# Clustered attention and a spatial gating unit on one core: the first pair by heads, casts on ScalarE, wider weight pieces, and a new planned order

## The chip, the cores and the metric

The kernel runs on one core of one Trainium2 chip. The engines are named as the profile names them: PE is TensorE (PEld its weight loads), DVE is VectorE, ACT is ScalarE, POOL is GpSimd, SP is SyncE, which here issues nearly all DMAs. The metric is the device time of one execution, in microseconds (us), and the median of several runs counts.

## The reference

There are 4 batches, 8 heads, 768 tokens and a head width of 64. Every query and key is given to the nearest of 16 centroids of its head (by cosine), and a query attends only to keys of its own cluster. What comes out is laid side by side by heads (512 wide) and goes through a gated unit.

```python
q_assign = argmax(einsum('bhsd,hcd->bhsc', q_n, c_n));  k_assign = the same with k_n
mask = q_assign[..., :, None] == k_assign[..., None, :]
scores = where(mask, 0.125 * q @ k.T, -1e9);  attn = softmax(scores)
x = (attn @ v), heads side by side            # 4 x 768 x 512
h = relu(x @ w_in);  u, v = h[..., :512], h[..., 512:]
v_n = (v - mean) / sqrt(var + 1e-6)           # over the 512 of one token
v_s = einsum('ts,bsd->btd', w_spatial, v_n) + b_spatial
out = (u * v_s) @ w_out
```

## The kernel before

Float32 values are carried as two float16 parts, a high part (a cast) and a low part (value minus high part), and a product is the sum of three products of parts. So each tensor that PE reads takes two steps, one for each part.

**Attention** goes by pairs of heads, n = 0 to 15, four pairs to a batch. `prep(n)` loads q and k of the pair (`raw`, one buffer), makes `hq` (ACT) and `lo` (DVE, line 592), takes the logits to the centroids on PE, and turns them on DVE into one-hot rows: maximum, comparison, code, maximum, comparison, then two scalings by the penalty (lines 631 and 632) into `ohx`. The one-hot rows reach `hq` by a DMA transpose and small DMAs, for the first pair by PE and two copies on DVE and two on ACT (line 652). `shifts(n)` computes scores of the own cluster for the maximum of every row (matmuls of line 716 into one of four PSUM accumulators `acc`, maxima on DVE, line 723); the maximum comes back as three more rows of `hq` by the transposes of line 746 and the DMA of line 747. `attend(n)` has twelve score tiles, six for each head: matmuls 767 and 769, the exponential 773 and the cast 775 on ACT, the low part 776 on POOL (`pt`), and 18 value matmuls, line 781. The head's result is divided (`rc`, `xn` on DVE), split into `xhl` (ACT and POOL) and transposed by DMA into `xT`.

**The gated unit** goes by 6 tiles of 128 tokens in each batch, `mlp(b)`. `v_tile` and `u_tile` multiply `xT` by the halves of `w_in` (12 matmuls of 512 columns each, line 826). Two `v` tiles share a chain of small steps for the root (lines 859 to 864: one on POOL, five on DVE), then they are scaled (866), cast (`vn`, 867, DVE) and split (868, POOL). `s_tile` multiplies by `w_spatial` (18 matmuls), gates (887), casts (`ghl`, 888, DVE), splits (889, POOL) and transposes by DMA (`gT`, 890). `p_tile` multiplies by `w_out` (12 matmuls); ACT takes the result out (897).

**Weights** are split too. `w_in` and `w_out` come as 64-bit values of which DVE makes float32 in three shifts (lines 526 to 528) before the high part (ACT, 504) and the low part (DVE, 511). `early_weights` loads all of `w_in` in eight pieces of 512 columns, with the shifts' result in an `acc`; `late_weights` loads `w_spatial` in twelve pieces of 384 columns and `w_out` in eight of 256, with the shifts' result in an SBUF tile `top`.

**The order** of every engine's queue is fixed when the kernel is built: all steps are recorded as operations with a cost, an engine and a key, and a planner (`Plan.run`) plays them through by its costs and lets the ready operation with the lowest due time plus key go first. `due()` gives the due times from the constants DUE_0, DUE, DUE_M and others; the keys are the constants with K_ and T_. At run time every engine works its queue off in that order and waits at the head for what is not there.

## Time and profile before

| what | value |
|---|---|
| median of 3 runs | 682.45 us (677.72 to 684.44) |
| profiled execution | span 679.7 us from the first to the last instruction; no time around the span is given |
| PE busy | 630.3 us, 93% of the span |
| DVE, ACT, POOL busy | 488.5, 418.7, 429.3 us |
| mean granted clock of PE | 0.992 |

The span of the profiled execution lies 2.75 us under the median of the timed runs and inside their spread. Busy PE counts each matmul from its start to its modelled end, so PE can be busy and still not run its matmuls back to back.

### The profile page before, as it was taken

What the parts mean: (1) busy time and instruction counts of PE and PEld (TensorE: products, weight loads), DVE (VectorE), ACT (ScalarE), POOL (GpSimd) and SP (SyncE); (2) the same over time, 40 slices, a digit from 0 to 9 for tenths busy, and PEclk for the clock granted to TensorE, in tenths of its full rate; (3) what the DMA queues carried; (4) which work ended last, traced back from release to release, by engine and by line L of the source; (5) the groups of instructions that cost most, each with busy time, mean ns of one, the idle gap of its engine ahead of it and who ended that gap; (6) DMA issues with size and microseconds to landing.
All of it is one profiled execution on the core that took longest, in us unless ns stands there. A gap on an engine that the chain in (4) does not pass through costs nothing.

```text
span 679.7 us, 16791 instructions
## 1 busy us (share of the span) xinstructions
PE 630.3 (93%) x6757; PEld 376.0 (55%) x6757; DVE 488.5 (72%) x937; ACT 418.7 (62%) x685; POOL 429.3 (63%) x305
## 2 busy tenths in 40 slices
...
GB/s 156 152 105 143 186 152 201 154 153 121 171 141 190 25 70 169 114 85 139 100 149 102 130 59 59 159 51 143 21 13 32 36 45 58 88 27 31 32 93 94
DMA packets 106515, 70.49 MB, mean 104 GB/s; under 512 B 90379, under 2 KB 93126, under 8 KB 106438
## 3 DMA queue, kind: packets, MB, share of 16 engines
...
## 4 chain that ended last, share of the span: by engine, by line
PE 53%; DVE 24%; DMA 11%; ACT 5%; issue 4%; POOL 1%; SPq 1%; POOLq 0%; DVEq 0%; ACTq 0%
PE acc L826 30%; DVE nm L723 8%; PE acc L781 8%; PE acc L716 5%; PE sc L767 5%; PE sc L769 5%; DMA raw<-in_kqT_dram 4%; DMA gT<-ghl 3%; DVE lo L592 2%; ACT p L773 1%; DVE vs L675 1%; ACT pt L775 1%; DMA vraw<-in_vp_dram 1%; DVE vhl L660 1%; DMA sht<-shx 1%
## 5 line engine op out<-in xcount | busy, mean ns | idle before, releaser
L776 POOL TENSOR_TENSOR pt<-p,pt 128x768 f16<-128x768 f32 x192 | 324.2, 1712 | 97.6 <-ACT pt L775 75.3
L723 DVE TENSOR_REDUCE nm<-acc 128x1 f32<-128x512 f32 (+1 forms) x288 | 182.4, 676 | 17.6 <-PE acc L716 17.4
L773 ACT ACTIVATE p<-sc 128x768 f32<-128x768 f32 x192 | 153.8, 809 | 44.8 <-PE sc L769 33.2
L775 ACT CAST pt<-p 128x768 f16<-128x768 f32 x192 | 157.4, 832 | 13.1 <-PE acc L781 10.4
L781 PEld LDWEIGHTS <-pt 128*128 128x128 f16 x3456 | 126.0, 97 | 25.2 <-POOL pt L776 2.4
L781 PE MATMUL acc<-vhl,pt 128*128 128x65 f16 (+1 forms) x3456 | 134.4, 193 | 1.9 <-POOL pt L776 1.9
L826 PE MATMUL acc<-win,xT 128*128 128x512 f16 x576 | 131.5, 379 | 0.4 <-DVE nm L723 0.4
L716 PE MATMUL acc<-hq 80*128 80x256 f16 (+1 forms) x384 | 100.6, 343 | 18.2 <-DVE nm L723 11.7
L767 PE MATMUL sc<-hq,lo 128*128 128x512 f16 (+1 forms) x384 | 95.6, 330 | 8.5 <-ACT p L773 8.1
L826 PE MATMUL acc<-vn,wsp 128*128 128x512 f16 x432 | 99.0, 379 | 0.0
L769 PE MATMUL sc<-hq 81*128 81x512 f16 (+1 forms) x384 | 95.5, 330 | 0.1
L826 PEld LDWEIGHTS <-xT 128*128 128x128 f16 x576 | 54.8, 98 | 63.1 <-issue 1.5
L826 PE MATMUL acc<-wou,gT 128*128 128x512 f16 x288 | 66.9, 379 | 1.8 <-DMA gT<-ghl 1.8
L826 PEld LDWEIGHTS <-wsp 128*128 128x128 f16 x432 | 41.0, 98 | 46.7 <-issue 0.4
L889 POOL TENSOR_TENSOR ghl<-u,ghl 128x512 f16<-128x512 f32 x24 | 28.3, 1178 | 51.6 <-DVE ghl L888 42.8
L887 DVE SCALAR_TENSOR_TENSOR u<-acc,bsp,u 128x512 f32<-128x512 f32 x24 | 17.9, 747 | 58.5 <-PE acc L826 58.5
L716 PEld LDWEIGHTS <-hq 80*128 80x128 f16 x384 | 35.2, 100 | 40.3 <-issue 19.7
L767 PEld LDWEIGHTS <-lo 128*128 128x128 f16 x384 | 35.1, 99 | 37.5 <-issue 21.6
L769 PEld LDWEIGHTS <-hq 81*128 81x128 f16 x384 | 37.8, 98 | 26.8 <-issue 1.9
L877 ACT ACTIVATE u<-acc 128x512 f32<-128x512 f32 x24 | 14.3, 596 | 54.6 <-PE acc L826 54.6
L805 POOL TENSOR_TENSOR xhl<-xn,xhl 128x384 f16<-128x384 f32 x32 | 31.6, 989 | 23.6 <-ACT xhl L804 22.5
L826 PEld LDWEIGHTS <-gT 128*128 128x128 f16 x288 | 27.7, 97 | 33.7 <-DMA gT<-ghl 2.3
(109 smaller groups left out, 645.6 us busy)
## 6 DMA issues: line engine op xcount, KB each, us to landing
...
```

Source lines behind the costliest of these rows:

```text
L716: T.matmul(out=acc.t[:, c:c + cs.stop - cs.start], lhsT=hq.t[0:R_SH, 1, h, t * P:(t + 1) * P], rhs=hq.t[0:R_SH, 0, h, cs], start=c == 0, s ...
L723: V.tensor_reduce(out=nm.t[:, t, k:k + 1] if n == 1 else nm.t[:, t:t + n, k], in_=src, axis=AX.X, op=ALU.max, negate=True)
L767: T.matmul(out=sc.t[:, cs], lhsT=lo.t[:, h, ks], rhs=hq.t[:, 2, h, cs], start=True, stop=False)
L769: T.matmul(out=sc.t[:, cs], lhsT=hq.t[0:R_E, 0, h, ks], rhs=hq.t[0:R_E, 1, h, cs], start=False, stop=True)
L773: o = op("ACT", 0.81, lambda sc=sc, p32=p32: A.activation(out=p32.t, in_=sc.t[:, 0:S], func=AF.Exp, bias=P_LOG * LN2, scale=SC_UNIT), afte ...
L775: o = op("ACT", 0.83, lambda pt=pt, p32=p32: A.copy(out=pt.t[:, 0, :], in_=p32.t), after=[o], use=[p32], new=[pt], key=K_HI)
L776: o = op("POOL", 1.72, lambda pt=pt, p32=p32: G_.tensor_tensor(out=pt.t[:, 1, :], in0=p32.t, in1=pt.t[:, 0, :], op=ALU.subtract), after=[o ...
L781: T.matmul(out=av.t[:, t * (D + 1):t * (D + 1) + w], lhsT=lhsT, rhs=rhs, skip_group_check=True, **f)
L805: xls.append(op("POOL", 1.0, lambda xn=xn, hs=hs: G_.tensor_tensor(out=xhl.t[:, :, 1, hs], in0=xn.t, in1=xhl.t[:, :, 0, hs], op=ALU.subtra ...
L826: T.matmul(out=acc.t, lhsT=lr[m][0], rhs=lr[m][1], start=(m == 0), stop=(m == n - 1))
L887: o = op("DVE", 0.72, lambda: V.scalar_tensor_tensor(out=u32.t, in0=acc.t, scalar=bsp[:, t:t + 1], in1=u32.t, op0=ALU.add, op1=ALU.mult), ...
L889: l = op("POOL", 1.2, lambda: G_.tensor_tensor(out=ghl.t[:, 1, :], in0=u32.t, in1=ghl.t[:, 0, :], op=ALU.subtract), after=[h], use=[u32, g ...
```

## The change

It has these parts:

- The first pair is prepared head by head: logits, maxima, one-hot rows and their transpose go once for each head, so that `hq` of head 0 doesn't wait for head 1. Of the copies of q under the one-hot rows, those for `hq[:, 1]` go by heads on ACT and the other by a DMA.
- The two scalings into `ohx` move from DVE to ACT for all pairs. The casts `vn` and `ghl` move from DVE to ACT.
- The chain for the root has one DVE step less.
- `w_out` is taken in four pieces of 512 columns with the shifts' result in an `acc`, `w_spatial` in six pieces of 768. The `u` half of `w_in` is loaded with the later weights. All these later weights share one buffer `wraw` of 1024 columns (before: three for `w_in`, two of 512 columns for the rest).
- `ghl` has two buffers instead of one, `gT` three instead of two.
- The costs of some DMAs in the planner and nearly all constants have new values, and so the order is another. Of that table two lines stand in the diff.

```diff
-DUE_MAX = -17.32
+DUE_MAX = -11.24
...
+GHL_BUFS = 2
+GT_BUFS = 3
...
-    r_wraw = R(wk, "wraw", [P, 512], F32, 2)
-    r_top = R(wk, "top", [P, 256], F32, 1)
+    r_wraw = R(wk, "wraw", [P, 1024], F32, 1)
...
-            top = tops.new()
+            top = r_acc.new()
...
+    def win_jobs(hf):
+        c0 = hf * DF
+        return [(w_in[k * P:(k + 1) * P, c0:c0 + DF], lambda k=k: win[:, :, k, c0:c0 + DF], DF, WIN_LOG, True, ("win", hf)) for k in range(NCT)]
 
     def early_weights():
...
+        return weights(win_jobs(1), W_AT, W_GAP, W_KEY, r_wraw0, "SP")
...
+        weights(win_jobs(0), WU_AT, WU_GAP, WU_KEY, r_wraw, "SP")
+        jobs = [(wsT[k * P:(k + 1) * P], lambda k=k: wsp[:, :, k], S, WS_LOG, False, "wsp") for k in range(NT)]
+        jobs += [(w_out[k * P:(k + 1) * P], lambda k=k: wou[:, :, k], DM, WOUT_LOG, True, "wou") for k in range(NDT)]
+        weights(jobs, WL_AT, WL_GAP, WL_KEY, r_wraw, "SP")
...
+        heads = [(0,), (1,)] if n == 0 else [(0, 1)]
         if n == 0:
-            qa0 = [op("ACT", 0.75, lambda x=x: A.copy(out=hq.t[0:D, x], in_=hq.t[D:P, 0]), after=his, use=[hq], key=KQ) for x in (1, 2)]
+            qa0 = [op("ACT", 0.75, lambda h=h: A.copy(out=hq.t[0:D, 1, h], in_=hq.t[D:P, 0, h]), after=[his[h]], use=[hq], key=KQ) for h in range(2)]
+            qa2 = [sp(lambda: nc.sync.dma_start(out=hq.t[0:D, 2], in_=hq.t[D:P, 0]), 0.9, after=his, use=[hq], key=KQ)]
...
-        k1 = op("DVE", 0.32, lambda: V.tensor_scalar(out=ohxv[:, :, 0:2], in0=oh2(0), scalar1=PEN, scalar2=None, op0=ALU.mult), after=[o_oh, last.get("oht"), c_oh], use=[misc], key=KA)
-        k2 = op("DVE", 0.32, lambda: V.tensor_scalar(out=ohxv[:, :, 2:4], in0=oh2(1), scalar1=PEN, scalar2=-PEN, op0=ALU.mult, op1=ALU.add), after=[o_oh, last.get("oht"), c_oh], use=[misc], key=KA)
...
+            k1 = op("ACT", 0.36 - 0.1 * one, lambda f=oh2, g=ohd: A.activation(out=g(0), in_=f(0), func=AF.Copy, scale=PEN), after=[o_oh, last.get("oht"), c_oh], use=[misc], key=KO)
+            k2 = op("ACT", 0.36 - 0.1 * one, lambda f=oh2, g=ohd: A.activation(out=g(1), in_=f(1), func=AF.Copy, scale=PEN, bias=-PEN), after=[o_oh, last.get("oht"), c_oh], use=[misc], key=KO)
...
-                h = op("DVE", 0.41, lambda t=t, v=v: V.tensor_copy(out=vn[:, 0, t, :], in_=v.t), after=[o] + vn_read[t], use=[v], key=T_NRM, port=True)
+                h = op("ACT", 0.6, lambda t=t, v=v: A.copy(out=vn[:, 0, t, :], in_=v.t), after=[o] + vn_read[t], use=[v], key=T_VH)
...
-            h = op("DVE", 0.43, lambda: V.tensor_copy(out=ghl.t[:, 0, :], in_=u32.t), after=[o], use=[u32], new=[ghl], key=T_G, port=True)
+            h = op("ACT", 0.6, lambda: A.copy(out=ghl.t[:, 0, :], in_=u32.t), after=[o], use=[u32], new=[ghl], key=T_G)
```

Three places show what the new order does. The first is ACT in the first pairs, from the second load of `raw` on (before) and from the one-hot scaling of the first head on (after). Before:

```order
L586 ACTIVATE hq<-raw 128x768 x2
L589 ACTIVATE raw<-raw 128x768 x2
L652 CAST hq<-sc_108 19x768 x2
L655 ACTIVATE vhl_88<-vraw 128x12x64
L686 ACTIVATE wl_93<-w_255 2x2x65
L657 ACTIVATE vraw<-vraw 128x768
L586 ACTIVATE hq<-raw 128x768 x2
L735 ACTIVATE shx_84<-nl 128x6
L738 ACTIVATE shx_84<-nl 128x6 x2
L773 ACTIVATE p_385<-sc_108 128x768
```

After:

```order
L643 ACTIVATE ohx<-acc_111 128x6x16
L644 ACTIVATE ohx<-acc_111 128x6x16
L650 CAST hq<-sc_108 19x768
L643 ACTIVATE ohx<-acc_111 128x6x16
L644 ACTIVATE ohx<-acc_111 128x6x16
L578 ACTIVATE hq<-raw 128x768 x2
L581 ACTIVATE raw<-raw 128x768 x2
L650 CAST hq<-sc_109 19x768
L657 ACTIVATE vhl_88<-vraw 128x12x64
L688 ACTIVATE wl_93<-w_271 2x2x65
L659 ACTIVATE vraw<-vraw 128x768
L737 ACTIVATE shx_84<-nl 128x6
```

The copy of the first head's rows stood behind the casts of the second pair's load, together with that of the second head, and now stands ahead of them by itself; the shift (`shx`) moved ahead of the third pair's casts.

The second place is DVE at the first piece of `w_out`, before from the step ahead of its second shift, after from its first shift. Before:

```order
L723 TENSOR_REDUCE nm_89<-acc_110 128x1
L527 SCALAR_TENSOR_TENSOR top<-wraw,top 128x256
L592 SCALAR_TENSOR_TENSOR lo<-raw,hq 128x768
L528 SCALAR_TENSOR_TENSOR top<-wraw,top 128x256
L887 SCALAR_TENSOR_TENSOR u_3332<-acc_112,bsp,u_3332 128x512
L511 SCALAR_TENSOR_TENSOR wou<-top,wou 128x256
```

After:

```order
L523 TENSOR_SCALAR acc_112<-wraw 128x512
L584 SCALAR_TENSOR_TENSOR lo<-raw,hq 128x768
L677 TENSOR_REDUCE vs<-vraw 128x128
L524 SCALAR_TENSOR_TENSOR acc_112<-wraw,acc_112 128x512
L631 TENSOR_REDUCE mx<-acc_111 128x24
L525 SCALAR_TENSOR_TENSOR acc_112<-wraw,acc_112 128x512
L632 TENSOR_TENSOR acc_111<-acc_111,mx 128x384
L888 SCALAR_TENSOR_TENSOR u_3112<-acc_110,bsp,u_3112 128x512
L633 TENSOR_TENSOR acc_111<-acc_111,wt 128x384
L509 SCALAR_TENSOR_TENSOR wou<-acc_112,wou 128x512
```

Four steps now make 512 columns where they made 256, through PSUM instead of SBUF, and one of the four accumulators is held from the first step to the last.

The third place is DVE at the first two `v` tiles of the third batch (`a`, `y`: the chain for the root). Before:

```order
L859 TENSOR_SCALAR a<-mv 128x2
L888 CAST ghl<-u_6672 128x512
L861 TENSOR_TENSOR y_7859<-y 128x2
L862 TENSOR_TENSOR y_7859<-y_7859,a 128x2
L863 TENSOR_SCALAR y_7859<-y_7859 128x2
L675 TENSOR_REDUCE vs<-vraw 128x128
L864 TENSOR_TENSOR y<-y,y_7859 128x2
L866 TENSOR_SCALAR v_7807<-v_7807,mv,y 128x512
L866 TENSOR_SCALAR v_7833<-v_7833,mv,y 128x512
L723 TENSOR_REDUCE nm_89<-acc_111 128x1
```

After:

```order
L861 TENSOR_SCALAR a<-mv 128x2
L863 SCALAR_TENSOR_TENSOR y_7923<-y 128x2
L864 TENSOR_TENSOR y_7923<-y_7923,a 128x2
L865 SCALAR_TENSOR_TENSOR y<-y_7923,y 128x2
L677 TENSOR_REDUCE vs<-vraw 128x128
L867 TENSOR_SCALAR v_7822<-v_7822,mv,y 128x512
L867 TENSOR_SCALAR v_7900<-v_7900,mv,y 128x512
L855 BN_STATS st<-v_8017 128x6
```

The cast into `ghl` is gone from DVE, and the chain is a step shorter.

## Rows read from the trace of the kernel before

**Rows 1.** The head of the page: the span, and busy us of each engine (share of the span) with the number of instructions.

```profile
span 679.7 us, 16791 instructions
...
PE 630.3 (93%) x6757; PEld 376.0 (55%) x6757; DVE 488.5 (72%) x937; ACT 418.7 (62%) x685; POOL 429.3 (63%) x305
```

**Rows 2.** Busy time by stage: start and end of the stretch, its length, busy us of PE, PEld, DVE, ACT and POOL (number of instructions), the granted clock of PE as a share of full speed, the busy share of the DMA engines, GB/s.

```profile
34.00:142.00 108.00, 94.72 (x1408) 66.32 (x1407) 101.86 (x191) 94.08 (x158) 88.91 (x56) 0.98 0.70 151
142.00:305.00 163.00, 155.04 (x1947) 97.89 (x1944) 155.42 (x276) 121.52 (x207) 125.35 (x82) 1.00 0.58 125
305.00:470.00 165.00, 163.89 (x1744) 97.06 (x1741) 129.53 (x238) 104.90 (x174) 107.32 (x74) 1.00 0.50 107
470.00:485.00 15.00, 12.52 (x92) 7.01 (x91) 12.38 (x17) 8.02 (x11) 7.57 (x5) 0.77 0.39 90
485.00:589.00 104.00, 104.00 (x1074) 61.05 (x1071) 42.31 (x89) 60.81 (x95) 71.75 (x51) 1.00 0.18 40
```

**Rows 3.** The timeline of the start: start us, duration us, engine, line, operation, tiles, count, and in brackets the idle time before it and what ended it.

```profile
9.29 0.96 DVE L592 SCALAR_TENSOR_TENSOR lo<-raw,hq 128x768 f16<-128x768 f32 x1
...
15.33 0.85 PE L635 MATMUL sc<-id,ohx 128*128 128x128 f16 x6
...
15.84 1.57 ACT L586 ACTIVATE hq<-raw 128x768 f16<-128x768 f32 x2 [3.37 <-DMA raw<-in_kqT_dram]
...
18.90 1.60 ACT L652 CAST hq<-sc 19x768 f16<-19x768 f32 x2
...
19.75 2.32 PE L716 MATMUL acc<-hq 80*128 80x512 f16 x6 [3.57 <-ACT hq L652]
...
20.39 3.08 DVE L723 TENSOR_REDUCE nm<-acc 128x1 f32<-128x512 f32 x5 [2.18 <-PE acc L716]
...
28.97 1.57 ACT L586 ACTIVATE hq<-raw 128x768 f16<-128x768 f32 x2 [6.66 <-DMA raw<-in_kqT_dram]
...
34.33 0.81 ACT L773 ACTIVATE p<-sc 128x768 f32<-128x768 f32 x1 [3.47 <-PE sc L769]
```

**Rows 4.** Groups of instructions by line and shape: count, busy us in all, mean ns of one, and the idle time ahead of them.

```profile
L592 DVE SCALAR_TENSOR_TENSOR lo<-raw,hq 128x768 f16<-128x768 f32 x30 | 41.2, 1377 | 3.4 <-ACT hq L586 3.4
...
L888 DVE CAST ghl<-u 128x512 f16<-128x512 f32 x24 | 18.9, 786 | 32.2 <-DMA gT<-ghl 32.0
...
L867 DVE CAST vn<-v 128x512 f16<-128x512 f32 x24 | 14.8, 653 | 0.0
...
L847 ACT ACTIVATE v<-acc 128x512 f32<-128x512 f32 x24 | 14.0, 594 | 37.2 <-PE acc L826 19.5 <-POOL vn L868 17.7
...
L511 DVE SCALAR_TENSOR_TENSOR wsp<-wraw,wsp 128x384 f16<-128x384 f32 x12 | 10.3, 858 | 1.4 <-ACT wsp L504 1.4
...
L511 DVE SCALAR_TENSOR_TENSOR wou<-top,wou 128x256 f16<-128x256 f32 x8 | 8.9, 1111 | 0.9 <-ACT wou L504 0.8
...
L528 DVE SCALAR_TENSOR_TENSOR top<-wraw,top 128x256 uint32<-128x256 uint32 x8 | 7.1, 888 | 0.1
...
L527 DVE SCALAR_TENSOR_TENSOR top<-wraw,top 128x256 uint32<-128x256 uint32 x8 | 6.4, 795 | 0.0
...
L526 DVE TENSOR_SCALAR top<-wraw 128x256 uint32<-128x256 uint32 x8 | 5.9, 744 | 0.0
...
L631 DVE TENSOR_SCALAR ohx<-acc 128x192 f16<-128x192 f32 x16 | 5.6, 348 | 0.1
...
L528 DVE SCALAR_TENSOR_TENSOR acc<-vn,acc 128x512 uint32<-128x512 uint32 x8 | 5.4, 678 | 0.0
```

**Rows 5.** Who PE waited for between 34 and 305 us: us in total, times, the longest.

```profile
PE sc L767 <- ACT p L773: 8.1, 18, 1.1
PE acc L716 <- DVE nm L723: 6.9, 20, 0.7
```

**Rows 6.** The timeline of PE in a stretch without a wait, for the price of matmuls back to back (columns as in rows 3).

```profile
578.15 1.25 PE L781 MATMUL acc<-vhl,pt 128*128 128x65 f16 x36
579.25 0.49 PE L767 MATMUL sc<-hq,lo 128*128 128x512 f16 x2
...
579.90 0.49 PE L767 MATMUL sc<-hq,lo 128*128 128x512 f16 x2
...
596.33 17.00 PE L826 MATMUL acc<-win,xT 128*128 128x512 f16 x78
```

**Rows 7.** The timeline around 474 us: DVE, then PE (columns as in rows 3).

```profile
470.09 0.43 DVE L888 CAST ghl<-u 128x512 f16<-128x512 f32 x1 [1.46 <-DMA gT<-ghl]
...
471.80 1.57 DVE L863 TENSOR_SCALAR y<-y 128x2 f32<-128x2 f32 x1
...
474.89 2.32 DVE L866 TENSOR_SCALAR v<-v,mv,y 128x512 f32<-128x512 f32 x2
...
477.86 0.59 PE L716 MATMUL acc<-hq 80*128 80x512 f16 x1 [2.48 <-DVE nm L723]
```

**Rows 8.** The timeline of the end: DVE, then PE (columns as in rows 3).

```profile
668.60 0.43 DVE L888 CAST ghl<-u 128x512 f16<-128x512 f32 x1 [1.32 <-DMA gT<-ghl]
...
673.43 2.76 PE L826 MATMUL acc<-wou,gT 128*128 128x512 f16 x12 [1.83 <-DMA gT<-ghl]
```

**Rows 9.** What DMA issues on SP waited for, over the whole span: us in total, times, the longest. L521 issues the loads of `w_in` and `w_out`.

```profile
SPq L521 <- DVE top L528: 9.5, 2, 8.5
...
SPq L521 <- DVE acc L528: 5.9, 1, 5.9
```

More of the change, by code (lines that the diff above doesn't have):

```diff
@@ L52 @@
 MM = 6
[L53 to L108 removed]
+W_KEY = 39.02
+WL_KEY = 33.98
+WU_KEY = 11.6
+WU_AT = 109.09
+WU_GAP = 8.81
+WL_AT = 69.05
+WL_GAP = 4.42
+W_AT = 57.96
+W_GAP = -36.25
+PREP_KEY = 13.33
+AV_KEY = 1.1
+K_SC = 11.08
+K_MX = -1.18
+K_MAX = 5.03
+TBL = 0.185
+K_SH = -40.3
+K_EXP = -100.66
+K_HI = -25.82
+K_LO = 161.1
+K_RC = 2.89
+K_XD = -29.01
+K_X = -35.23
+K_VT = -29.14
+K_G = -66.37
+KP0 = -8.82
+KC = -230.91
+T_LO = 4.55
+T_QA = 17.5
+T_OH = 6.67
+T_VH = 126.21
+T_LG = -126.86
+T_AM = -49.58
+T_OT = -3.67
+T_ROW = 14.27
+T_V = -13.63
+T_SV = 23.5
+T_VA = 2.23
+T_SA = 37.55
+T_SB = 1.67
+T_UO = 2.53
+T_PO = 47.91
+T_CONT = -98.96
+T_BN = -10.16
+T_NRM = -3.1
+T_VL = -197.16
+T_G = -39.45
+T_GL = -79.29
+T_O = 92.53
+T_B1 = 6.31
+T_B2 = 11.85
+T_B3 = 14.47
+T_Q1 = -2.89
+T_Q2 = -1.35
+T_Q3 = -3.86
+T_Q0 = -3.63
+T_Z0 = -3.86
+T_Z1 = -5.36
+T_Z2 = 17.86
 LO_POOL = (1,)
+LO0_POOL = ()
 VL_POOL = (0, 1)
 SUM_PE = tuple(range(4))
[L112 removed]
 O_BUFS = 1
+GHL_BUFS = 2
+GT_BUFS = 3
 class Ring:
@@ L631, in prep @@
-        k1 = op("DVE", 0.32, lambda: V.tensor_scalar(out=ohxv[:, :, 0:2], in0=oh2(0), scalar1=PEN, scalar2=None, op0=ALU.mult), after=[o_oh, last.get("oht"), c_oh], use=[misc], key=KA)
-        k2 = op("DVE", 0.32, lambda: V.tensor_scalar(out=ohxv[:, :, 2:4], in0=oh2(1), scalar1=PEN, scalar2=-PEN, op0=ALU.mult, op1=ALU.add), after=[o_oh, last.get("oht"), c_oh], use=[misc], key=KA)
-        if n == 0:
-            tp = r_sc.new()
-            tr = op("PE", 0.4, lambda: [T.matmul(out=tp.t[:, t * P:(t + 1) * P], lhsT=ohx[:, t].rearrange("p x c -> p (x c)"), rhs=id16, start=True, stop=True) for t in range(NT)], after=[k1, k2, c_id], new=[tp], cols=S, key=KP)
-            last["oht"] = tr
-        else:
-            tr = last["oht"] = sp(lambda: nc.sync.dma_start_transpose(oht.t, ohx.rearrange("p t x c -> p (t x c)")), 0.67, after=[k1, k2], new=[oht], turn=True, key=KP + T_OT)
@@ L639, in prep @@
-        rows = []
-        for x in range(4) if n else (0, 2, 1, 3):
-            m = (C if n else R_END - R_OH) if x > 1 else C + 1
-            def dst(x=x, m=m):
-                return hq.t[R_OH:R_OH + m, x // 2, x % 2, :]
-            def src(x=x, m=m):
-                if n == 0:
-                    return tp.t[2 * x * C:2 * x * C + m, 0:S]
-                return oht.t[2 * x * C:2 * x * C + m].rearrange("c t s -> c (t s)")
-            if n == 0:
-                rows.append(op(("DVE", "ACT")[x // 2], 0.9, lambda dst=dst, src=src, x=x: (V.tensor_copy, A.copy)[x // 2](out=dst(), in_=src()), after=[tr, lg] + qa0, use=[hq, tp], key=KR))
-            else:
-                rows.append(sp(lambda dst=dst, src=src: nc.sync.dma_start(out=dst(), in_=src()), 0.1, after=[tr, lg] + qa0, use=[hq, oht], key=KR))
+        ohxv = ohx.rearrange("p t (x e) c -> p t x e c", e=2)[:, :, :, 0, :]
@@ L688, in prep @@
         w2 = sp(lambda: nc.sync.dma_start(out=mw.t[R_E + 1:R_E + 2, :, 0:D + 1], in_=wl.t[0:1, :, 0:D + 1]), 0.05, after=[l_, c_mean], use=[wl, mw], key=KS)
-        X["rows"] = [(rows if n else rows[2 * h:2 * h + 2]) + qa0 for h in range(2)]
-        X["go"] = rows + qa0 + [qa1, lo1]
+        X["rows"] = [rows[2 * h:2 * h + 2] + [qa0[h]] if n == 0 else rows + qa0 for h in range(2)]
+        X["go"] = [x + qa2 + [qa1, lo1] for x in X["rows"]]
         X["v"] = [o_vh, o_vl, w1, w2]
@@ L769, in scores @@
                         T.matmul(out=sc.t[:, cs], lhsT=hq.t[0:R_E, 0, h, ks], rhs=hq.t[0:R_E, 1, h, cs], start=False, stop=True)
-                o = last["sc"] = op("PE", 0.66, scores, after=X["go"] + [X["shift"][h], last.get("sc")] + exps[-2:-1], use=[hq, lo], new=[sc], cols=2 * S, key=K_SC)
+                o = last["sc"] = op("PE", 0.66, scores, after=X["go"][h] + [X["shift"][h], last.get("sc")] + exps[-2:-1], use=[hq, lo], new=[sc], cols=2 * S, key=K_SC)
                 o = op("ACT", 0.81, lambda sc=sc, p32=p32: A.activation(out=p32.t, in_=sc.t[:, 0:S], func=AF.Exp, bias=P_LOG * LN2, scale=SC_UNIT), after=[o, m_half], use=[sc], new=[p32], key=K_EXP)
```

192 lines of the change are left out of this document (70 added, 122 removed).

## The prediction

> **What bounds the kernel now.** I read the head of the page first: PE is busy for 93% of the span, DVE for 72% [rows 1]. That average hides two regimes, which the table by stage shows [rows 2]. From 34 to 305 us DVE is the full engine: 101.86 of 108 us and 155.42 of 163, while PE stands still for 13.3 and 8.0. From 305 to 470 DVE is at 129.53 of 165 and PE at 163.89; from 485 to 589 PE never stops. So the second half is bound by PE, and only the first half, the start, one disturbance and the end can give time.
>
> How much idle the first half hides follows from prices of matmuls back to back [rows 6]: a matmul of 512 columns takes 17.00/78 = 0.216, a score tile 0.65 (start of one to start of the next), a block of 18 value matmuls 0.55 (36 in 1.25 less the last one's tail). Counted in PE's order between the last values of pair 3 (142 us) and of pair 8 (305 us), before has 58 score tiles, 60 value blocks, 90 blocks for maxima and 234 matmuls of the gated unit: 37.7 + 33 + 19.4 + 50.5, and about 7 of small ones, 147.6 us. The stretch lasts 163, so some 15 us are slack; PE's waits say for whom: the exponential on ACT (8.1 from 34 to 305) and the maxima on DVE (6.9) [rows 5].
>
> **The change, part by part.** The order's counts are mine; durations are from the rows.
>
> *Start.* Today the first maximum's matmul waits for the copies of both heads' rows (18.90 to 20.50, the matmul at 19.75); they stand on ACT behind casts of pair 1, which waited until 15.84 for their load [rows 3]. By heads: `lo` of head 1 ends at 10.25, the first head's one-hot is the seventh of ten half steps (0.35 as line 631, which has the same 192 elements) and ends at 12.7, two scalings at ACT to about 13.4, the transposes 0.85, a copy 0.8: 15.1, so 4.6 earlier [rows 3, 4]. But the first exponential (34.33) stays behind the casts of pair 2 on ACT, whose load landed at 28.97 with casts of 1.57 [rows 3]. `raw` has one buffer and comes free no sooner, and on SP a copy into `hq` now goes ahead of this load. I put the first exponential at 31.3: **3.0 us gained**, bounds 0 and 4.6.
>
> *Pairs 0 to 3 (34 to 142).* DVE does 7 weight steps of 0.68 less (24 for 31, `u` half later), 12 one-hot scalings of 0.35 less and, by the new order, 5 maxima of 0.62 more [rows 3, 4]: -4.8 - 4.2 + 3.1, so 96 for 101.9. ACT takes those scalings (14 with the halves; no row has one on ACT; between the 0.35 of DVE and, above, the 0.594 of an ACT step on 512 columns; I take 0.35 for a full one, it is the nearer size) and one cast less: 94.1 + 3.8 = 98. ACT is then the fuller engine. At today's filling of the fullest, 101.86/108 = 0.943, 98 needs 104: **4 gained**, bounds -4 (ACT's 14 us of idle all stay) and 6.
>
> *Pairs 4 to 8 (142 to 305).* DVE loses 10 scalings (3.5), 6 casts `vn` at 0.653 (3.9), 3 casts `ghl` at 0.786 (2.4); `w_out` goes from 19 steps of 0.74 to 1.11 (16.6) to 16 of 0.68 (10.9); `w_spatial` from 12 at 0.858 (10.3) to 6 at 1.38, as `lo` of the same shape (8.3) [rows 4]. It gains 7 more steps of `w_in` (4.8). Steps of other pairs and tiles that change sides make about -2.4. In all -15: 140 us. PE gets more to do there: 56 score tiles, 60 blocks, 86 for maxima, and 408 matmuls of the gated unit for 234, 182 us by the same prices. So DVE goes from 95% to 77% of the stretch, PE has filler, and the bound turns over to PE, as from 305 to 470 where DVE at 78.5% left PE 1.1 us idle [rows 2]. Of 15 us of slack I let 4 stand: **11 gained**, bounds 0 and 15. The cover is that filler; without it the freed DVE time buys nothing. An `acc` is now held through a piece of `w_out`, which is in the 4 that I leave.
>
> The `vn` and `ghl` casts cost ACT 0.594 each where an undisturbed DVE cast takes 0.43 [rows 4, 7]. The Trainium skill, page "ScalarE: Activation LUTs", section "Rules for kernel authors", says to keep plain arithmetic on VectorE, being faster per element there; undisturbed, the trace agrees. By that rule the 16 casts up to pair 8 would cost 2.6 us more engine time, and the stage would gain some 3 less. But the mean of the casts on DVE is 0.786 and 0.653 here [rows 4], for DVE works beside a busy POOL, and DVE is the full engine, so I don't take it.
>
> *The disturbance at 474.* A cast `ghl` waits 1.46 on DVE for the one buffer, which a transpose still reads; behind it the small step L863 takes 1.57 and the scalings 2.32, and PE waits 2.48 for a maximum [rows 7]. The stage's granted clock falls to 0.77 [rows 2]: (1 - 0.77) x 15 = 3.4 us, as 6.9 us at the lower level of 1.2 GHz, after PE had stood still for 2.48. Together 5.9. With two buffers, the cast on ACT and a chain without L863 all but POOL's neighbourhood is gone: **5 gained**, bounds 0 and 5.9.
>
> *The end.* The last cast waits 1.32 for the same buffer, and PE 1.83 for the last `gT` [rows 8]. The cast on ACT takes 0.17 longer: **1 gained**, bounds 0 and 1.8.
>
> *New stalls.* An order written anew has places of its own like that at 474; there is one in some 340 us today. I charge one: **5 lost**, bounds 0 and 12.
>
> Other edits cost nothing visible: the chain's step less is off PE's path except at 474; third `gT` and larger pieces lie beside PE's filler.
>
> Sum: 3 + 4 + 11 + 5 + 1 - 5 = 19. From the span of 679.7 that is 660.7; the median lies 2.75 above the span, so **663 us**, 2.8% faster.
>
> **The rivals.** *ACT takes DVE's place.* For: from 34 to 142 it is at 94.08 already [rows 2], its queue gets waits on DVE's chains ahead of exponentials, and PE waits for those longest [rows 5]. Against: its share falls to 121.52 of 163 afterwards. Then pairs 0 to 3 lose 4 and pairs 4 to 8 gain half: 3 - 4 + 5.5 + 5 + 1 - 5 = 5.5, or 677.
>
> *One `wraw` buffer blocks SP (slower).* Each of the 14 later loads (4 + 6 + 4) must wait until the one before is landed and read, at the head of SP's queue, with the shift's transposes behind it. Two loads waited 9.5 us in all, the longer 8.5, and another 5.9 [rows 9]; the shifts' due time moved from -17.32 to -11.24, so 6 us of lead that covered such a wait are gone. If three loads hold SP for 5.9 where no lead is left, PE loses 18; with no gain from pairs 0 to 8, 4 remain: 682.45 - 4 + 18 = 696. It decides from the second bare hold on. Against: the loads start earlier, and the first use of `w_spatial` comes more than a pair after its last piece in DVE's order.
>
> *All slack goes.* Every upper end, no new stall: 4.6 + 6 + 15 + 5.9 + 1.8 = 33, or 649. For: stages after 305 have next to none [rows 2].
>
> That the change doesn't do what it says can only be at the start, where the third load sets the exponential; that is the lower end there.
>
> **How the numbers follow.** Chances: the forecast 0.60, ACT as the bound 0.17, SP blocked 0.10, all slack gone 0.13. A measurement of this kernel can't tell changes under about 1% from none. The forecast and the last case are faster; ACT as the bound lies within 1% for the most part; SP blocked is slower. That makes 0.75, 0.14 and 0.11. The range goes from 648, the last case, to 683, which takes in the ACT case with the lower ends of the start and the disturbance; outside stay SP blocked and little else.
>
> **What would show it.** Right: the first exponential at 30 to 32; the last values of pair 3 by 136; from there to pair 8's end PE idle under 4 us and DVE under 85% of the stretch; no clock below 1.00 between 300 and 600; PE's last wait for `gT` under 1 us. Wrong: ACT busy over 95% with PE waiting for exponentials (first rival), SP standing at `wraw` loads while PE waits for scores (second), or a new stall of 10 us and more in the second half.

## The result and the profile after

The changed kernel takes 661.76 us (661.38 to 662.23 in four executions) against 681.12 (677.72 to 684.44, four) for the kernel before on the same chip: 0.9729 of its time, 95% interval 0.9684 to 0.9774. The forecast was 663.0. The profiled execution took 662.23, its span is 660.5. Of the experiments, one of e10's four executions took 1622.92 us and is left out of its median.

The head of the page after, and the shares of the chain of work that ended last, by engine (answers to [rows 1]):

```profile
span 660.5 us, 16716 instructions
...
PE 623.7 (94%) x6763; PEld 374.4 (57%) x6763; DVE 423.6 (64%) x828; ACT 446.7 (68%) x757; POOL 426.2 (65%) x305
...
PE 75%; DVE 12%; issue 6%; ACT 4%; DMA 1%; POOL 1%; POOLq 0%; SPq 0%; ACTq 0%; DVEq 0%
```

DVE lost 65 us of work, ACT took 28. The stages (columns as in [rows 2]; 137.7 is the end of pair 3's last values, 330 that of pair 8's):

```profile
34.00:64.00 30.00, 25.28 (x375) 17.13 (x373) 24.07 (x46) 21.59 (x41) 18.73 (x13) 0.93 0.56 133
64.00:137.70 73.70, 67.08 (x1055) 47.80 (x1052) 72.25 (x133) 71.12 (x123) 69.25 (x43) 1.00 0.73 169
137.70:330.00 192.30, 187.81 (x2081) 112.39 (x2080) 148.03 (x272) 138.41 (x240) 132.76 (x90) 1.00 0.56 127
330.00:476.00 146.00, 146.00 (x1700) 90.71 (x1697) 98.23 (x177) 110.91 (x186) 106.62 (x74) 1.00 0.49 107
476.00:590.00 114.00, 113.89 (x1123) 66.04 (x1121) 43.16 (x97) 69.96 (x112) 73.59 (x54) 1.00 0.20 42
```

From 64 to 137.7 DVE is still the full engine (98%, with ACT at 96.5%). From there to 330 it is at 77%, PE stands 4.5 us in 192, and from 330 to 590 it stands for 0.1.

Where the time came from can't be read by comparing pairs, since the new order puts 174 more matmuls of the gated unit ahead of pair 8's end. So I compared the traces at equal work: for a moment of the changed kernel I added up the columns of all matmuls that PE had started, and looked up when the kernel before had started as many.

| the changed kernel at | share of all columns | before at | lead, us |
|---|---|---|---|
| 30.6 (first exponential) | 1.2% | 35.5 | 4.9 |
| 64.2 (end of pair 0) | 4.9% | 62.7 | -1.5 |
| 137.7 (end of pair 3) | 15.0% | 144.7 | 7.0 |
| 330.0 (end of pair 8) | 45.5% | 343.9 | 13.9 |
| 455 | 66.1% | 469.3 | 14.3 |
| 480 | 70.3% | 500.2 | 20.2 |
| 650 | 99.2% | 669.4 | 19.4 |

The lead at the start is gone by the end of pair 0, some 1.6 us of it at a stretch from 45.3 to 48.7 us in which the granted clock is 0.50 (see e8); 8.5 come from pairs 1 to 3 (1.8 of them because the kernel before had a stretch of 3.4 us at the lower clock there, at 68 us), 6.9 from pairs 4 to 8, 5.9 at the disturbance, and the end takes 0.8 back.

### The profile page after: what moved, and what is told of

Its sections match the earlier page's. It is cut to its first block, busy times and chain, and to the rows that moved or that the text cites. A ratio compares the mean times of both kernels' runs of the same rounds, so it can differ in the third digit from the quotient of the medians.

```text
span 660.5 us, 16716 instructions
## 1 busy us (share of the span) xinstructions
PE 623.7 (94%) x6763; PEld 374.4 (57%) x6763; DVE 423.6 (64%) x828; ACT 446.7 (68%) x757; POOL 426.2 (65%) x305
## 4 chain that ended last, share of the span: by engine, by line
PE 75%; DVE 12%; issue 6%; ACT 4%; DMA 1%; POOL 1%; POOLq 0%; SPq 0%; ACTq 0%; DVEq 0%
PE acc L828 38%; PE acc L783 13%; PE sc L769 7%; PE sc L771 7%; DVE nm L725 7%; PE acc L718 6%; ACT p L775 2%; ACT pt L777 1%; DMA raw<-in_kqT_dram 1%; PE acc L613 1%; PE acc L614 1%; DMA gT<-ghl 1%; PE acc L612 1%; DVE mx L631 1%; POOL pt L778 1%
## 5 line engine op out<-in xcount | busy, mean ns | idle before, releaser
L828 PE MATMUL acc<-win,xT 128*128 128x512 f16 x576 | 129.1, 379 | 0.5 <-DVE nm L725 0.5
L718 PE MATMUL acc<-hq 80*128 80x256 f16 (+1 forms) x384 | 96.3, 335 | 8.6 <-DVE nm L725 7.0
L828 PE MATMUL acc<-vn,wsp 128*128 128x512 f16 x432 | 97.6, 379 | 0.0
L889 ACT CAST ghl<-u 128x512 f16<-128x512 f32 x24 | 14.8, 618 | 52.0 <-DVE u L888 52.0
L718 PEld LDWEIGHTS <-hq 80*128 80x128 f16 x384 | 33.0, 99 | 24.4 <-issue 10.1
```

What stands on the lines that cost most here:

```text
L718: T.matmul(out=acc.t[:, c:c + cs.stop - cs.start], lhsT=hq.t[0:R_SH, 1, h, t * P:(t + 1) * P], rhs=hq.t[0:R_SH, 0, h, cs], start=c == 0, s ...
L828: T.matmul(out=acc.t, lhsT=lr[m][0], rhs=lr[m][1], start=(m == 0), stop=(m == n - 1))
```

## The experiments

In all but e5 the order of the kernel that the experiment starts from was written out as a list and replayed, so that one part is changed and every other instruction keeps its place in its queue; an instruction that must wait for one further down the list moves behind it. Line numbers in rows of these kernels are shifted. The sets ran on other chips; the kernel before had medians of 677.71, 678.40, 678.11 and 677.34 there. The changed kernel ran on the first chip alone, where the kernel before took 681.12, so a comparison of times with 661.76 goes across chips. Variants are still compared with it directly, for e4 and e8, which differ from it least, gave 661.92 and 661.31 in two of these sets, and e4's trace runs 0.1 to 0.2 us beside the changed kernel's from pair 0 to the end. Where it matters the neighbour in the same set is named too.

### e1 and e2: single parts in the kernel before

```diff
-    r_ghl = R(moe, "ghl", [P, 2, DF], F16, 1)
-    r_gT = R(moe, "gT", [P, 2 * NDT, P], F16, 2)
+    r_ghl = R(moe, "ghl", [P, 2, DF], F16, 2)
+    r_gT = R(moe, "gT", [P, 2 * NDT, P], F16, 3)
```

> The kernel before with its own order of instructions on every engine, word for word, and only two buffers for ghl (for one) and three for gT (for two). Theory 1 (the stall near 474 us hangs on the one buffer: the cast waits 1.46 us, behind it the small step and the scalings come late, PE stands 2.48 us and then runs 6.9 us at the lower clock level): no wait of the cast for a transpose there, no stage with a granted clock below 1.00 near 474, 4 to 6 us faster than before, so 675 to 677. Theory 2 (the neighbourhood of POOL slows the small step and the scalings, whatever the cast does): at most 1.5 us faster, and the granted clock still falls after 470.

675.95 us, 0.9966 of before (0.9941 to 0.9991). The stage of the disturbance, then the cast and the small step on DVE:

```profile
470.00:485.00 15.00, 14.86 (x166) 9.44 (x164) 14.87 (x24) 12.68 (x20) 11.12 (x7) 1.00 0.41 83
```
```profile
467.64 0.42 DVE L932 CAST ghl<-u 128x512 f16<-128x512 f32 x1
...
469.97 1.50 DVE L907 TENSOR_SCALAR y<-y 128x2 f32<-128x2 f32 x1
```

The cast waits no more, PE is busy 14.86 of 15 us for 12.52 in [rows 2], and the clock stays at 1.00, although the small step still takes 1.50. At equal work the lead rises from 0.9 to 6.3 us there, as theory 1 says. But the median gains 1.8 only, and 11 of the 19 executions of the kernel before in this set have a mean clock of 0.997 or more, where 6.8 us at 0.50 would leave 0.995: most of them don't pay this stall in full. Its size was a property of the execution that was profiled. And since an execution of the kernel before can go without it, one profile of each doesn't show that the buffers alone took it away: e2, with one `ghl` buffer and the casts off DVE, has a clock of 1.00 there too.

```diff
-h = op("DVE", 0.43, lambda: V.tensor_copy(out=ghl.t[:, 0, :], in_=u32.t)
+h = op("ACT", 0.6, lambda: A.copy(out=ghl.t[:, 0, :], in_=u32.t)
```

(and the same for `vn` and the two scalings)

> The kernel before with its own order, and the casts of vn and ghl and the one-hot scalings on ACT, each in the place that its old time gives it; nothing else of the change. Theory 1 (from 34 to 305 us DVE is the full engine, so what is taken from it shows at once): DVE's busy time from 142 to 305 falls from 155 to some 146 and the run is 4 to 8 us faster, 674 to 678. Theory 2 (the new order, which brings 174 more matmuls of the gated unit ahead of pair 8's end, is what fills PE; the casts alone only move the wait from DVE to ACT): within 1.5 us of before.

680.03 us, 1.0029 of before (1.0006 to 1.0052). Two of the stages of [rows 2], and the group of `ghl` casts on ACT:

```profile
142.00:305.00 163.00, 153.11 (x1893) 96.16 (x1892) 148.17 (x254) 125.80 (x223) 121.53 (x81) 1.00 0.56 123
305.00:470.00 165.00, 160.54 (x1733) 95.60 (x1732) 115.17 (x210) 111.80 (x194) 103.29 (x73) 1.00 0.47 104
```
```profile
L932 ACT CAST ghl<-u 128x512 f16<-128x512 f32 x24 | 14.8, 617 | 45.2 <-DMA gT<-ghl 28.3 <-DVE u L931 16.9
```

DVE is 7 us freer from 142 to 305, and PE does no more for it (153.11 for 155.04). ACT now stands 28.3 us at the head of its queue for the one `ghl` buffer, with exponentials behind. Freeing DVE in this way is worth nothing in the old order with one `ghl` buffer; both edits together in that order were not run.

### e3, e4 and e11: single parts taken out of the changed kernel

e3 puts the casts and scalings back on DVE (e2's edit reversed).

> The changed kernel with its own order, and the casts of vn and ghl and the one-hot scalings back on DVE, each in its place. Theory 1 (freed DVE time is a good part of the gain): pairs 0 to 3 lose 2 to 3 us, since DVE is busy 72 of 74 us there already, pairs 4 to 8 another 2 to 3: 665 to 668. Theory 2 (PE's filler hides what DVE does from pair 4 on, and the scalings cost DVE no more than the wait for ACT): within 1.5 us of the changed kernel, 660 to 663.3.

665.02 us, 0.9807 of before (0.9752 to 0.9863), 3.3 slower than the changed kernel and 3.1 slower than e4 in the same set: theory 1, at its lower end. From 138 to 330, the changed kernel first, then e3:

```profile
138.00:330.00 192.00, 187.51 (x2079) 112.21 (x2078) 147.72 (x271) 138.10 (x240) 132.46 (x90) 1.00 0.56 127
```
```profile
138.00:330.00 192.00, 187.90 (x2080) 112.88 (x2079) 156.56 (x302) 129.71 (x214) 132.89 (x91) 1.00 0.56 129
```

8.8 us more on DVE change nothing for PE in this stage: filler hides them, as theory 2 says for it. In the profiled execution 1.9 us were lost by 158 us, ahead of the first cast `vn` (166.1), so none of it is the casts'; its first exponential comes at 32.40 for 30.64, with the scalings on DVE. Some 1 comes back by 210, and 1.5 go again between 330 and 570, where the casts can be the cause.

```diff
-        heads = [(0,), (1,)] if n == 0 else [(0, 1)]
+        heads = [(0, 1)]
```

> The changed kernel with its own order, and the first pair's one-hot codes made for both heads in one piece again (one group of logits, five steps, two scalings, one group of transposes) in the place of the second head's. Theory 1 (the start's 3.7 us, seen at the first exponential, are not carried: the second pair's maxima start at 39.6 us for 40.0 before, since that pair's codes are no earlier): the first exponential falls back to 32.5 to 34.5, the second pair's first maximum stays within 1 us of 39.6, and the end is within 1 us of the changed kernel, 661 to 663. Theory 2 (the start is carried to the end): 3 to 4 us slower, 665 to 666.

661.92 us, 0.9778 of before (0.9711 to 0.9844). ACT at the start, the changed kernel first, then e4:

```profile
15.50 0.79 ACT L650 CAST hq<-sc 19x768 f16<-19x768 f32 x1 [0.98 <-PE sc L647]
...
16.59 1.58 ACT L578 ACTIVATE hq<-raw 128x768 f16<-128x768 f32 x2
...
30.64 0.81 ACT L775 ACTIVATE p<-sc 128x768 f32<-128x768 f32 x1 [0.49 <-PE sc L771]
```
```profile
16.02 0.79 ACT L701 CAST hq<-sc 19x768 f16<-19x768 f32 x1 [0.92 <-PE sc L696]
...
30.75 0.81 ACT L826 ACTIVATE p<-sc 128x768 f32<-128x768 f32 x1
```

The end is where theory 1 put it, but its own number for the start was wrong too: the first exponential moved by 0.1 us, not by 2 to 4. Making the codes by heads is worth nothing that can be measured (the copies of the rows still go by heads in e4). The timelines say what brought the first exponential from 34.33 [rows 3] to 30.64: on ACT the first row copy now stands ahead of the second pair's four casts (15.50 and 16.02 for 18.90 before), and the shift ahead of the third pair's (25.10 for 30.45). The scalings on ACT have a part in it, for e3 without them has 32.40. No run took the order on ACT back alone.

```diff
-GHL_BUFS = 2
-GT_BUFS = 3
+GHL_BUFS = 1
+GT_BUFS = 2
```

> The changed kernel with its own order, and one buffer for ghl and two for gT as in the kernel before. Theory 1 (in the new order, too, the cast of the next tile would wait for the transpose of the last, now on ACT with exponentials behind it): waits of 1 us and more on ACT at the casts of ghl, and 1 to 4 us slower, 663 to 666. Theory 2 (with MLP tiles spread evenly the buffers are idle long enough): within 1 us, 660.8 to 662.8.

672.46 us, 0.9886 of before (0.9842 to 0.9931): 10.7 slower, far beyond theory 1. One row of who ACT waited for (us, times, longest), which the changed kernel doesn't have:

```profile
ACT ghl L934 <- DMA gT<-ghl: 21.9, 5, 6.8
```

At equal work 13.5 us go between 245 and 299 us, in pair 7: the cast holds ACT, and the exponentials and casts `pt` behind it come late. PE then waits 6.3 us, and after that its granted clock is down:

```profile
PE acc L828 <- POOL pt L823: 6.3, 3, 3.6
```
```profile
266.00:283.10 17.10, 14.68 (x94) 8.64 (x95) 7.91 (x15) 8.77 (x15) 8.93 (x7) 0.50 0.15 38
```

By estimate the lower clock costs half of the 14.68, which is 7.3, and with the 6.3 that makes the loss. Two buffers that are worth 1.8 us in the old order carry 10.7 in this one, which was planned with them; a new order for one buffer was not tried.

### e5, e6 and e7: the order

```diff
-DUE_PREP = -73.77
-W_AT = 57.96
+DUE_PREP = -59.83
+W_AT = 71.02
```

(and every other number that both tables have)

> The changed code with every number of the table that both kernels have set to its value in the kernel before, so that the order is planned from the old numbers; the eight that only the changed kernel has, and all its casts, scalings, pieces and buffers, stay. Theory 1 (the new table is more than half of the gain: the parts alone gave about 2 us with the buffers and 3 us with the casts): 668 to 674. Theory 2 (the parts make the gain and any sensible order of them does): within 2 us of the changed kernel, 660 to 664.

690.53 us, 1.0186 of before (1.0158 to 1.0214). Every other part of the change is in it, and it is 12 us slower than before and 29 slower than with its own table (29 slower than e8 in the same set, too). From 64 to 300 us PE waits 11.3 us for exponentials, the changed kernel 4.8:

```profile
PE sc L769 <- ACT p L775: 11.3, 18, 2.5
```
```profile
PE sc L769 <- ACT p L775: 4.8, 11, 0.8
```

The parts need a table that fits them; how much of the 29 is this table's merit and how much the old one's misfit, the run can't say.

```diff
-        weights(win_jobs(0), WU_AT, WU_GAP, WU_KEY, r_wraw, "SP")
+        weights(win_jobs(0), WU_AT, WU_GAP, WU_KEY, r_wraw0, "SP")
```

(and the place of these instructions in the list)

> The changed kernel with its own order for all but one part: the u half of w_in (four pieces: loads, twelve steps and four lo steps on DVE, four casts on ACT) stands where the kernel before has it in time, right behind the v half and through the same three buffers. Theory 1 (from 64 to 138 us DVE is busy 72.25 of 73.7, so 7 to 8 steps of 0.6 to 0.68 us more show one to one there, and pairs 4 to 8 get less back, since PE bounds them): 3 to 5 us slower, 665 to 667. Theory 2 (DVE's steps for weights slip into its idle time, and the third pair's end stays): within 1 us of the changed kernel, 661 to 663.

669.18 us, 0.9872 of before (0.9839 to 0.9906): 7.4 slower than the changed kernel, 7.9 slower than e8 in the same set, theory 1 but more of it. At equal work the loss lies between 114 and 162 us, 7.6 us, where 7 to 8 steps of 0.68 make 5. PE and DVE at 142 us show a part of the rest:

```profile
142.11 0.38 PE L763 MATMUL acc<-hq 80*128 80x512 f16 x1 [0.78 <-DVE nm L770]
143.27 0.38 PE L763 MATMUL acc<-hq 80*128 80x512 f16 x1 [0.78 <-DVE nm L770]
```
```profile
142.52 0.69 DVE L770 TENSOR_REDUCE nm<-acc 128x1 f32<-128x512 f32 x1 [0.47 <-PE acc L763]
143.68 0.69 DVE L770 TENSOR_REDUCE nm<-acc 128x1 f32<-128x512 f32 x1 [0.47 <-PE acc L763]
144.29 0.68 DVE L554 SCALAR_TENSOR_TENSOR win<-acc,win 128x512 f16<-128x512 f32 x1
```

Matmul and maximum wait for each other in turn, 1.16 us for one maximum of 0.69: one of the four `acc` is left for them, another is held by the piece of `w_in` until 145.0. So a weight piece costs its steps and, on top, the `acc` that it holds. How much of the 2.6 that is can't be told from the run, for the granted clock is 0.50 here from 134.6 to 138.0 and from 144.9 to 148.3.

```diff
-order of the 24 instructions of w_out: casts wou on ACT from 224.2 to 255.1
+order of the 24 instructions of w_out: casts wou on ACT from 306.7 to 337.1
```

> The changed kernel with its own order for all but one part: the four pieces of w_out (loads and steps) stand 85 us later, so that the last is ready at about 340 us as in the kernel before (345) and not at 256; the output projections of the first batch can only follow it. Theory 1 (what filled PE in pairs 4 to 8 are the 174 more matmuls of the gated unit that an early w_out lets run there): PE idle comes back there, and the run is 4 to 8 us slower, 666 to 670. Theory 2 (DVE's relief does it, and the filler may as well run later): within 1.5 us of the changed kernel, 660 to 663.3.

683.96 us, 1.0086 of before (1.0057 to 1.0115): 22.2 slower than the changed kernel, 22.7 slower than e8 in the same set. From 225 to 345 us, the changed kernel, then e7:

```profile
225.00:345.00 120.00, 119.64 (x1261) 70.47 (x1258) 80.95 (x151) 83.26 (x143) 76.22 (x53) 1.00 0.58 126
```
```profile
225.00:345.00 120.00, 109.36 (x1159) 64.69 (x1158) 80.02 (x148) 77.04 (x132) 72.75 (x50) 0.96 0.46 109
```

DVE does the same work in both, two thirds of the stage; PE stands 10.6 us and does 102 matmuls less. So theory 1: what fills PE in pairs 4 to 8 is work that exists because `w_out` is ready, and a free DVE alone is not the gain. In the kernel before the first output projection started at 345.8 us, in the changed one at 257.9. But the 22.2 are not all for want of filler. At equal work 10 go between 249 and 289 us, where value blocks wait for POOL's `pt` and the clock is at 0.50 from 260.2 to 267.0. The other 11 to 12 go between 307 and 365, where the late projections stand in a heap and PE waits for them:

```profile
337.73 14.34 PE L873 MATMUL acc<-wou,gT 128*128 128x512 f16 x57 [2.02 <-ACT wou L553]
355.13 4.45 PE L873 MATMUL acc<-wou,gT 128*128 128x512 f16 x12 [3.06 <-DMA gT<-ghl]
```

Whether the filler needed the freed DVE isn't shown: with 8.8 us more on DVE (e3) PE lost nothing in this stage.

### e8, e9 and e10: where the lead of the start went

```diff
+                    for _ in range(14):
+                        T.matmul(out=r_sc.tiles[1][:, 0:512], lhsT=id16, rhs=hq.t[:, 0, 0, 0:512], start=True, stop=True)
...
-                    for t, cs, c in parts:
+                    for t, cs, c in parts * (2 if twice else 1):
```

> The changed kernel with its own order, and more for PE at the start whose results are not used: 14 matmuls of 512 columns into a free score buffer behind the first logits (where PE stood 3.7 us), and each of the nine groups for the first head's maxima done twice over. In the changed kernel the granted clock was at the lower level from about 21.4 to 35.1 and 45.3 to 48.7 us. Theory 1 (the low clock lies beside waits for DVE and ACT and costs nothing; runs of the changed kernel at a mean clock of 0.987 and 0.994 had the same time): within 1 us, 660.8 to 662.8, whatever the clock does. Theory 2 (the low clock is what took back the 3.7 us of the start): the granted clock is 1.00 in the first 60 us and the run is 2 to 4 us faster, 658 to 660.

661.31 us, 0.9755 of before (0.9725 to 0.9785): by time theory 1, though the clock didn't do what theory 2 asks for. PE by stretches of 3 us (its busy time, granted clock, DMA share, GB/s): full from 12 to 15, where the changed kernel has 0.34, and yet at the lower level of 1.2 GHz from 30 to 33 (28.3 to 35.1 in all).

```profile
12.00:15.00 3.00, 3.00 (x9) 1.00 0.97 294
...
30.00:33.00 3.00, 3.00 (x11) 0.50 0.59 121
```

Up to 34 us the clock costs nothing that these traces show. The changed kernel and e11, whose order is the same up to there, were at 0.75 and 0.73 from 9 to 34; e7 was at 1.00, and yet it stands 0.4 us behind the changed kernel at the first maximum (19.34 for 18.92) and still 0.3 behind it at 44 us. First e11, then e7:

```profile
9.00:34.00 25.00, 18.28 (x141) 10.67 (x138) 21.89 (x43) 14.07 (x27) 8.04 (x5) 0.73 0.67 175
```
```profile
9.00:34.00 25.00, 19.02 (x147) 10.95 (x147) 21.89 (x44) 14.74 (x28) 7.60 (x5) 1.00 0.65 172
```

Behind that it does cost. In the changed kernel the granted clock is 0.50 from 45.3 to 48.7, with PE busy throughout; in e7 and e11 it is 1.00 there. Two rows of the same maxima on DVE stand around this stretch, in the changed kernel and then in e7:

```profile
45.30:48.70 3.40, 3.40 (x26) 2.11 (x26) 2.66 (x7) 1.58 (x2) 0.00 (x0) 0.50 0.33 65
```
```profile
44.54 2.04 DVE L725 TENSOR_REDUCE nm<-acc 128x1 f32<-128x512 f32 x3
52.72 0.68 DVE L725 TENSOR_REDUCE nm<-acc 128x1 f32<-128x512 f32 x1
```
```profile
44.85 1.87 DVE L770 TENSOR_REDUCE nm<-acc 128x1 f32<-128x512 f32 x3
51.39 0.68 DVE L770 TENSOR_REDUCE nm<-acc 128x1 f32<-128x512 f32 x1
```

Ahead of it the changed kernel leads by 0.3, behind it it lags by 1.3: 1.6 us lost, and against e11 and e12 it is 1.6 as well. That is most of what moves the end of pair 0 (64.2 in the changed kernel; 61.8, 62.9 and 63.0 in e11, e7 and e12). From there on the gap stays as it is: at the end of pair 3 these three are 2.4, 1.3 and 1.2 ahead, e11 is still 2.4 ahead at the end of pair 6 and e12 1.2 at the end of pair 15. So what is gained by the end of pair 0 is carried through, though DVE and ACT are 96 to 98% busy behind it.

Not all of the lead gets there: e7 has its first exponential 3.3 us ahead of the kernel before (31.06 for 34.33) and its end of pair 0 only 1.0 ahead (62.9 for 63.9), with no low clock in either. The trace shows one reason: DVE stands still before the third pair's logits, with the second pair's maxima behind them. In the changed kernel:

```profile
39.82 0.56 DVE L631 TENSOR_REDUCE mx<-acc 128x24 f32<-128x384 f32 x1 [3.56 <-PE acc L614]
```

```diff
-PE: ... score tile, value block, third pair's logits, maxima, maxima ...
+PE: ... third pair's logits, maxima, maxima, score tile, value block ...
```

> The changed kernel with its own order but for three groups on PE: the third pair's logits and the first two of the second pair's maxima stand ahead of the score tile and the value block that they followed (DVE stood still from 36.3 to 39.8 us there, waiting for these logits, which waited behind value blocks for POOL). Theory 1 (at the start the end of pair 0 is set by when DVE gets its next work, not by the first exponential): the wait of 3.6 us on DVE falls to 1 to 1.5 us, the third pair's end comes 1 to 2.5 us earlier than 137.7 and the run is 1 to 2 us faster, 659.5 to 661. Theory 2 (PE and ACT set the pace there and DVE's wait was beside them): within 0.5 us of the changed kernel.

663.27 us, 0.977 of before (0.9725 to 0.9815): 1.5 slower than the changed kernel, which neither theory said.

```profile
37.37 0.56 DVE L676 TENSOR_REDUCE mx<-acc 128x24 f32<-128x384 f32 x1 [1.98 <-PE acc L659]
```

The wait fell from 3.56 to 1.98, pair 0 ended at 62.4, the lead of 1.8 us held to the end of pair 2 (111.7 for 113.5) and was lost in pair 3 (137.5 for 137.7). There the granted clock is down with PE busy throughout:

```profile
119.20:122.60 3.40, 3.40 (x26) 1.93 (x25) 2.92 (x5) 3.40 (x8) 2.62 (x2) 0.50 0.49 111
```

The changed kernel is at 1.00 there, and e8, which also falls to 0.50 from 120.5 to 123.9, loses 1.5 us at the same place. So up to 119 us the profiled execution speaks for theory 1, at half of its price (0.9 of the 1.8 stood at the first maximum already, 18.05 for 18.92, ahead of the edit), and then the clock took that back. Why the median lies above that execution (662.09) isn't shown; the mean clocks of the four, 0.982 to 0.990, are on the whole below those of the changed kernel, 0.987 to 0.994.

```diff
-            if n in LO_POOL or (n == 0 and h in LO0_POOL):
+            if n in LO_POOL and h:
+                plan.seq += 1
+            elif n in LO_POOL:
```

(and 28 places in the list)

> The changed kernel with its own order but for the second pair's codes: lo of its second head on DVE straight from the load (for a cast on ACT and a subtraction on POOL), its logits, the five steps, the two scalings and the transpose ahead of the last five of the first pair's first nine maxima, and its own first maxima some 2 to 4 us earlier on PE and DVE. Theory 1 (the start's gain was lost because the second pair's codes were no earlier than in the kernel before): the second pair's first maximum comes at 35 to 38 us for 40.3, the first exponential 2 to 3 us later, and the run is 0 to 2.5 us faster, 659 to 662. Theory 2 (the first exponential is what counts after all): 2 to 3 us slower, 664 to 665.

664.71 us, 0.9778 of before (0.9727 to 0.983). By time that is theory 2, but the edit didn't do what it was to do: the second pair's first maximum came at 39.25 (expected 35 to 38), because DVE waited 2.04 us for its matmul. It says nothing for either theory, save that this order isn't better.

### e12: the end

```diff
-            o32 = r_o32.new()
+            o32 = (r_v32 if b == B - 1 and t == NT - 2 else r_o32).new()
```

(and the store behind the next copy in the list)

> The changed kernel with its own order, but at the very end the store of the last tile but two is issued behind the copy of the next tile (which goes to a free v buffer so that it needn't wait for the store), some 2 to 3 us later. In the changed kernel this store was issued at 650.25, 0.5 us behind the end of POOL's part of the last ghl (649.78), and the two transfers ran side by side from 651.0 to 653.4; PE waited 1.9 us for the last gT. Theory 1 (the store takes transfer time from the last transpose, which is why the end gained nothing though the wait for the ghl buffer is gone): PE's last wait falls to 1.0 to 1.4 us, and the end comes 0.5 to 0.9 us earlier. Theory 2 (the transpose takes that long by itself): the wait stays at 1.8 to 2.0.

660.39 us, 0.9754 of before (0.9713 to 0.9796). The end of the changed kernel, then of e12:

```profile
648.62 1.16 POOL L890 TENSOR_TENSOR ghl<-u,ghl 128x512 f16<-128x512 f32 x1 [5.32 <-ACT ghl L889]
...
650.25 0.40 ACTq L899 DMA_DIRECT2D out_dram<-o  x1
...
654.10 2.76 PE L828 MATMUL acc<-wou,gT 128*128 128x512 f16 x12 [1.92 <-DMA gT<-ghl]
```
```profile
647.47 1.16 POOL L935 TENSOR_TENSOR ghl<-u,ghl 128x512 f16<-128x512 f32 x1 [5.32 <-ACT ghl L934]
...
651.06 0.34 ACTq L944 DMA_DIRECT2D out_dram<-o  x1
...
651.78 2.76 PE L873 MATMUL acc<-wou,gT 128*128 128x512 f16 x12 [0.76 <-DMA gT<-ghl]
```

From POOL's end to PE's start it is 4.32 us with the store 0.47 behind POOL's end, 3.15 with the store out of the way. Theory 1, and a little more than it expected: the wait falls to 0.76, the end gains 1.2 us. PE's row is 2.3 us earlier than in the changed kernel; the other 1.2 is the lead that this execution has from the end of pair 0 on (see e8) and not the edit's. This version has the lowest median of all, but its interval overlaps that of the changed kernel.

## Why the prediction was right, and where its steps were wrong

**The sum** of 19 met the 19.4 of the profiled execution, with errors that cancel. By the borders of the prediction's terms and at equal work: start 4.9 for 3, pairs 0 to 3 2.1 for 4, pairs 4 to 8 6.9 for 11, disturbance 5.9 for 5, end -0.8 for 1, no new stall of its own for the 5 lost, and 0.4 in between. That the time met the forecast within 1.3 us is luck in part: 663 adds 2.75 to the span where the profiled execution lies 1.7 above its own, and on the other chips the kernel before takes 677 to 678, against which 661.76 would be a gain of 16 only. Two slips in the working change nothing: 17.00/78 is 0.218 and not 0.216, and the ACT case with the two lower ends comes to 685 and lies outside the range.

**Start.** The first exponential came at 30.64 (30 to 32 forecast, 31.3 in the sum), so the size was right. The cause named, going by heads, is not: e4 has the same time without it, and the order on ACT and the scalings there are what the timelines show. What the term lacked is what comes behind it, for by the end of pair 0 the lead is -1.5: DVE stands 3.56 us for the third pair's logits (e9), and in the profiled execution 1.6 us go at the low clock.

**Pairs 0 to 3.** DVE's work from 34 us on was to be 96 and is 96.3 (24.07 and 72.25). But ACT was to be the fuller engine with 98 and has 92.7 (21.59 and 71.12), and that the filling of the fullest stays at 0.943 failed: from 34 to 64 us DVE is busy 24.07 of 30, where the kernel before has 28.54 of 29.9 up to its end of pair 0. So the term's 2.1 is made of 6.4 lost up to the end of pair 0 and 8.5 gained behind it, neither of them forecast, and each kernel loses some 1.7 at a stretch at the lower clock, the changed one at 45 us, the one before at 68. The end at 137.7 missed the mark "by 136". The sign for the first rival, ACT over 95% with PE waiting for exponentials, does show from 64 to 137.7 (96.5%, PE waits 3.9 us), but not its price.

**Pairs 4 to 8.** That filler is what PE lacked holds, by e7. DVE's share came out as said, 77%; that the filler needed it so low isn't shown (e3 has it at 82% and PE as full). The size failed at the slack: 15 us by back-to-back prices, of which the trace showed 8.0 as idle time [rows 2]. The other 7 were matmuls that take longer in this mixture than those prices say, and they still do: 6.9 were gained, with 4.5 idle left (under 4 forecast).

**The rule against casts on ACT.** The casts take 0.618 on ACT (the undisturbed one on DVE took 0.43 [rows 7]), as this group of the changed kernel shows:

```profile
L889 ACT CAST ghl<-u 128x512 f16<-128x512 f32 x24 | 14.8, 618 | 52.0 <-DVE u L888 52.0
```

The Trainium skill's rule, page "ScalarE: Activation LUTs", section "Rules for kernel authors", to keep plain arithmetic on VectorE, holds here for the single undisturbed instruction. The trace of the kernel before shows what its mean of 0.786 on DVE hides: 14 of the 24 `ghl` casts took 0.42 to 0.43 us, with POOL idle or at work beside them for 0.2 at most, and eight took 1.13 to 1.86 with POOL at work all along. The small step L863 takes 0.17 or, in the same way, 1.09 to 1.58. For the kernel as a whole the runs don't decide: with the scalings, casts on DVE cost 3.3 us (e3), but the larger part of that is lost before the first of them runs, and in the order of before moving them brought nothing (e2).

**Disturbance.** Right in size for the execution profiled, and in cause as far as e1 shows it; no granted clock below 1.00 came between 49 and 659 us. Too large for the median, where e1 gained 1.8.

**End.** The buffer wait of 1.32 went, as said. PE's last wait was still 1.92 (under 1 forecast): the last transpose now met a store, which I hadn't looked for (e12). In the kernel before the store had been issued 0.57 ahead of POOL's end, and POOL's end to PE's start was 3.18. The term lacked the question what the released transfer runs into.

**New stalls.** None of 5 us came. By e11 the second `ghl` buffer prevents one of 10.7 in this order; the 5 charged for bad luck were not needed.

**The rivals.** SP stood at the late loads through `wraw` 4.9 us at most for one waiter, 1.9 the longest, and no wait of PE is put down to it. ACT in DVE's place is what e2 and e11 show, when the buffers or the order are not there.
